# Sparse attention and two expert layers on one core: batch 0's softmax statistics for two heads at a time

## The chip, the cores and the metric

The kernel runs on one core of one Trainium2 chip. The metric is the device time of one execution in microseconds. Three runs of the kernel before took 711.41, 712.30 and 712.85 us, a median of 712.3 us.

## The reference

Inputs are in float32 for q, k, v (2 batches, 8 heads, 576 rows, 64 columns); the weights of the two layers behind the attention follow. The attention keeps in each row only the scores within tau of the row's largest:

```python
scores = scale * np.matmul(q, k.transpose(0, 1, 3, 2))
thresh = np.max(scores, axis=-1, keepdims=True) - tau
scores = np.where(scores >= thresh, scores, -1000000000.0)
scores = scores - np.max(scores, axis=-1, keepdims=True)
attn = np.exp(scores)
attn = attn / (np.sum(attn, axis=-1, keepdims=True) + 1e-09)
return np.matmul(attn, v).astype(np.float32)
```

Its output, 1152 tokens of 512 numbers, goes through a layer `max(x @ w1, x @ w2, x @ w3) @ w_out` and then through four experts of 1024 hidden units, whose outputs are summed with the normalised probabilities of each token.

## The kernel before

The program has two halves. Batch 0's attention comes first and alone on TensorE (`attention_fast`, L531); the products of the two layers (L1192) start behind it, and batch 1's attention (`attention_slow`) is woven into them piece by piece. The change is in `attention_fast` and in the functions that it calls.

**Tiles.** Batch 0 has four jobs, each a pair of heads. A job has nine tiles (`job_steps`, L322): 128 rows of scores against 576 keys, for four chunks of rows and two heads, and one tile with the 64 remaining rows of both heads (`st.h` is None there). The tiles of a chunk follow one another, head 0 and then head 1 (its `mate`), and share one buffer `em`. The 36 tiles are numbered through, from 0. Jobs 0 and 3 have the remainder before their last two tiles, jobs 1 and 2 at their start, so the remainders are tiles 6, 9, 18 and 33.

**One tile.** `qk` (L344) puts the scores into `s` in PSUM, four matmuls of 288 columns; there are two such buffers. `peak` (L369) takes the row's negated maximum on VectorE, `limit` (L376) the threshold from it, on one column. `power` (L379) takes the exponential on ScalarE, into `em`. `weigh` (L383) masks it on VectorE by comparing `s` with the threshold, and sums the row; with it the score buffer is free. `norm` (L389) takes the reciprocal of the sum on VectorE and multiplies the row with it on GpSimd (the last tiles on VectorE). `turn` (L399) transposes the tile on TensorE, four transposes into `t` (two buffers), and for a chunk's second head or a remainder a fifth into `tm`. `cut_hi`, `cut_lo` and `cut_late` split the transposed tile into a high and a low part: in mode "pe" (head 0) by ScalarE, a second set of transposes, a product with the negative identity (L456) and ScalarE again, in mode "pool" (head 1) by a copy on ScalarE and two operations on GpSimd, for a remainder on VectorE. `gather` (L467) multiplies with the values when a group of chunks is complete. `prep` (L198) prepares the next job's keys and queries, one step at each call of `advance`.

**Order.** The loop at L557 writes these steps in program order, for tile `i`: its maximum, the reciprocal of tile `i - 1`, the scores of `i + 1`, the exponential, threshold and mask of `i`, the transposes of `i - 1`, with the splitting of `i - 2` in between. In this half a scheduler then orders each engine's instructions by its own estimate of times; behind it the order on TensorE, VectorE, ScalarE and GpSimd is the program's. Each engine works through its list in order and waits where an operand is not there.

In the listing, the names of buffers are those of the profile: `st_negm`, `st_thr`, `st_sum`, `st_r` are the four columns of a tile (L373).

Of the kernel before, what the change touches and what calls it, by code (L numbers as in the profile page):

```python
# [11 lines left out]
F32 = mybir.dt.float32  # L12
# [3 lines left out]
ALU = mybir.AluOpType  # L16
# [6 lines left out]
def fused_kernel(ctx: ExitStack, tc: tile.TileContext, q, k, v, tau, w1, w2, w3, w_out, probs, m_w1, m_w2, out):  # L23
    nc = tc.nc
# [3 lines left out]
    E, _, F2 = m_w1.shape  # L28
    P = 128
# [28 lines left out]
    SWIFT = 2  # L58
# [3 lines left out]
    CALM, NEARLY = 3, 6  # L62
# [82 lines left out]
    def atile(shape, dt, tag):  # L145
        return at["pool"].tile(shape, dt, tag=tag, name=tag, bufs=at["bufs"].get(tag, 1))

    def ptile_at(x, shape):
        return at[x].tile(shape, F32, tag=x, name=x.lower())

    def load_job(job, names="qkv"):
        b, p = job.b, job.p
        for nm, src in (("q", q), ("k", k), ("v", v)):
            if nm not in names:
                continue
            heads = src[b, 2 * p:2 * p + 2]
            load = nc.scalar.dma_start if nm == "v" and b else nc.sync.dma_start
            main = heads[:, 0:MAIN, :].rearrange("h (p c) d -> p h c d", c=NC)
            if nm == "v":
                t = atile([P, 2, NC, D], F32, "vnat")  # L160
                load(out=t, in_=main)
            else:
                t = atile([P, NC, 2, D], F32, f"{nm}nat")
                for h in range(2):
                    nc.sync.dma_start(out=t[:, :, h, :], in_=main[:, h])
            if nm == "q":
                r = diagonal
                for h in range(2):
                    last = nc.sync.dma_start(out=r[h * REM:(h + 1) * REM, h * D:(h + 1) * D], in_=heads[h, MAIN:S, :])
            elif nm == "k":  # L170
                r = atile([REM, 2, D], F32, "knrem")
                last = nc.sync.dma_start(out=r, in_=heads[:, MAIN:S, :].rearrange("h r d -> r h d"))
            else:
                r = atile([P, D], F32, "vnrem")
                last = load(out=r, in_=heads[:, MAIN:S, :])
            job.raw[nm] = (t, r)
        return last
# [13 lines left out]
    def spin(ps, n):  # L191
        for _ in range(n):
            nc.tensor.matmul(ps, lhsT=still[:, 0:P], rhs=still, start=True, stop=True)  # L193
# [128 lines left out]
    def job_steps(job):  # L322
        steps = []
        late = job.b == 0 and job.p in (0, NPAIR - 1)
        groups = (((0, 1), False), ((2, 3), True))
        for chunks, with_rem in groups if late else groups[::-1]:
            grp = Step()
            grp.job, grp.chunks = job, chunks
            grp.nn = len(chunks) * P
            grp.n = grp.nn + (REM if with_rem else 0)  # L330
            grp.am = [None, None]

            tiles = [(ci, c, h) for ci, c in enumerate(chunks) for h in range(2)]
            if with_rem:
                tiles.insert(-2 if late else 0, (None, None, None))
            for ci, c, h in tiles:
                st = Step()
                st.grp, st.ci, st.c, st.h, st.last = grp, ci, c, h, False
                st.mate = steps[-1] if h else None
                steps.append(st)  # L340
            steps[-1].last = True
        return steps
# [26 lines left out]
    def peak(st):  # L369

        st.em = st.mate.em if st.mate else atile([P, 2 * S], F32, "em")
        st.col = (st.h or 0) * S
        st.stat = {x: atile([P, 1], F32, f"st_{x}") for x in ("negm", "thr", "sum", "r")}  # L373
        nc.vector.tensor_reduce(out=st.stat["negm"], in_=views(st)[0], op=ALU.max, axis=AX.XY, negate=True)  # L374

    def limit(st):  # L376
        nc.vector.tensor_scalar(out=st.stat["thr"], in0=st.stat["negm"], scalar1=-1.0, scalar2=ntau, op0=ALU.mult, op1=ALU.add)

    def power(st):  # L379
        sv, _, ev = views(st)  # L380
        return nc.scalar.activation(out=ev, in_=sv, func=AF.Exp, bias=st.stat["negm"])  # L381

    def weigh(st):  # L383

        sv, _, ev = views(st)
        nc.vector.scalar_tensor_tensor(  # L386
            out=ev, in0=sv, scalar=st.stat["thr"], in1=ev, op0=ALU.is_ge, op1=ALU.mult, accum_out=st.stat["sum"])

    def norm(st, swift=False):  # L389
        em = views(st)[1]  # L390
        su, re = st.stat["sum"], st.stat["r"]
        nc.vector.reciprocal(out=re, in_=su)  # L392
        last = (nc.vector if swift else nc.gpsimd).tensor_scalar(out=em, in0=em, scalar1=re, scalar2=one, op0=ALU.mult, op1=ALU.mult)  # L393
        if st.h is None:
            nc.gpsimd.tensor_scalar(
                out=st.em[:, S:S + REM], in0=st.em[:, MAIN:S], scalar1=1.0, scalar2=1.0, op0=ALU.mult, op1=ALU.mult)
        return last

    def turn(st):  # L399
        st.t = ptile_at("T", [P, NC, P])  # L400
# [62 lines left out]
    def cut_late(st):  # L463
        if st.mode == "pe":
            st.late()
# [65 lines left out]
    def attention_fast(jobs, modes):  # L531

        steps = lined_up(jobs)
        n = len(steps)
        front, back = Queue(), Queue()
        spin(ptile_at("S", [P, 2, 512])[:, 0, 0:SPUN], SPINS)
        load_first(jobs[0])
        stream.flush(-55000)
        load_job(jobs[0], "v")
        start = prep_first(jobs[0])  # L540
        next(start)
        qk(steps[0])
        for _ in start:
            pass
        stream.flush(-READY)
        back.add(values(jobs[0]))

        def advance():

            with ExitStack() as held:  # L550
                if "raised" in at:
                    held.enter_context(tc.issue_after(at["raised"].ins))
                front.advance()
                back.advance()

        urgent = ExitStack()
        for i in range(n + 3):  # L557
            st = steps[i] if i < n else None
            nxt = steps[i + 1] if i + 1 < n else None
            old = steps[i - 2] if 0 <= i - 2 < n else None  # L560
            if st and st.j + 1 < len(jobs):
                if st.r == 0:
                    load_job(jobs[st.j + 1], "v" if st.j else "qkv")
                if st.r == 1 and st.j == 0:
                    front.add(prep(jobs[1]))
                if st.r == AHEAD_A and st.j + 2 < len(jobs):
                    load_job(jobs[st.j + 2], "qk")
            if st:
                peak(st)
            if 0 <= i - 1 < n - 1:  # L570
                norm(steps[i - 1], i - 1 >= n - SWIFT)
            if nxt:
                if nxt.r == 0:
                    front.drain()
                    back.add(values(nxt.job))
                qk(nxt)
                if nxt.r == 0 and nxt.j + 1 < len(jobs):
                    front.add(prep(jobs[nxt.j + 1]))
                if i < len(SPINS_A):
                    with tc.issue_after(nxt.whole.ins):  # L580
                        spin(ptile_at("U", [P, SPUN]), SPINS_A[i])
            if st and not nxt:
                power(st)
                limit(st)
                weigh(st)
                at["normed"] = norm(st, True)
                turn(steps[i - 1])
                urgent.enter_context(tc.issue_after(at["normed"].ins))
            if old:
                cut_hi(old, next(modes) if old.h is not None and i - 2 < n - CALM else "dve")  # L590
            advance()
            if nxt:
                at["raised"] = power(st)
                if i == n - NEARLY:
                    at["nearly"] = at["raised"]
            if old:
                cut_lo(old)
            if nxt:
                limit(st)
            advance()  # L600
            if nxt:
                weigh(st)
                if i:
                    turn(steps[i - 1])
            if st and not nxt:
                at["turned"] = turn(st)
            if old:
                cut_late(old)
                if old.last:
                    back.add(gather(old.grp, i - 2 == n - 1))  # L610
            advance()
            yield
        back.drain()
        urgent.close()
        at["fourth"] = at["stacked"]
# [611 lines left out]
    bufs_a = {"K12": 2, "QS": 2, "V": 2, "VR": 2, "em": 3, "am": 6, "ar": 4}  # L1227
    bufs_b = {"sraw": 2, "K12": 2, "QS": 2, "em": 2, "am": 4, "ar": 2}
    for bf in (bufs_a, bufs_b):
        bf.update({f"st_{x}": 6 for x in ("negm", "thr", "sum", "r")})  # L1230

    layer_max(0)
    MAX0 = plan.cols
# [105 lines left out]
```

## Time and profile before

| | |
|---|---|
| median of three runs | 712.3 us |
| lowest and highest run | 711.41 and 712.85 us |
| profiled execution, its own time | 713.38 us |
| its span from the first to the last instruction | 711.6 us |
| TensorE busy | 693.5 us, 97% |
| VectorE busy | 470.5 us, 66% |
| ScalarE busy | 359.3 us, 50% |
| GpSimd busy | 494.7 us, 70% |

The busy shares are means over the whole program. In the page's 40 slices of 17.8 us the digit of VectorE is 6 in the first slice, then 8, 9, 9, 8, 9, that of TensorE 7 and then 9 throughout; the granted clock of TensorE is 8 tenths in the first slice and 9 or more from the second. Batch 0's attention lies in the first six slices. Instruction times below are in microseconds from the start of the span. VectorE's instructions are pipelined a little: the next one starts before the end of the one before, so the step from start to start is shorter than the duration.

### The profile page before, as it was taken

How to read it: one execution, taken by the hardware profiler on the slowest of the kernel's cores; microseconds unless marked ns; L12 is line 12 of the kernel's file. 1: busy time of each engine (PE TensorE's matmuls, PEld its weight loads, DVE VectorE, ACT ScalarE, POOL GpSimd, SP SyncE). 2: the span in 40 equal slices, each digit the busy share in tenths (PEclk: the TensorE clock that was granted, in tenths of full speed). 3: DMA queues.
4: the chain of work that ended last, by engine and by line, in shares of the span. 5: the costliest groups of instructions: out<-in, count | busy, mean ns of one | idle time of the engine just before them, and what ended most of it. 6: DMA issues, size and time to landing. Idle time of an engine off the chain costs nothing.

```text
span 711.6 us, 11870 instructions
## 1 busy us (share of the span) xinstructions
PE 693.5 (97%) x3961; PEld 613.8 (86%) x3961; DVE 470.5 (66%) x1050; ACT 359.3 (50%) x760; POOL 494.7 (70%) x575
## 2 busy tenths in 40 slices
PE   7999999999899999999999999999999999999997
PEld 7878888877688888888878889999998998998996
DVE  6899898776476676677666477874744644643653
ACT  5788875553454465464555344446524433434430
POOL 5769976876585665675676567789479669669650
PEclk8999999999999999999999999999999999999999
DMA  6763507987978358365333544443232223222203
GB/s 190 177 145 83 152 1 201 277 228 225 238 196 215 119 154 214 106 167 155 119 103 97 178 169 149 148 157 125 60 90 72 78 87 90 87 65 90 56 1 75
DMA packets 108176, 95.04 MB, mean 134 GB/s; under 512 B 26708, under 2 KB 91220, under 8 KB 108116
## 3 DMA queue, kind: packets, MB, share of 16 engines
q1 hardware_dynamic: 90218, 81.14, 40.6%
q10 hardware_dynamic: 17866, 13.14, 6.5%
q8 instruction: 32, 0.52, 0.3%
q14 instruction: 28, 0.23, 0.1%
q0 software_dynamic: 32, 0.00, 0.0%
HBM read 68.96 MB, written 13.37 MB: 116 GB/s over the span
## 4 chain that ended last, share of the span: by engine, by line
PE 84%; ACT 4%; POOL 3%; DVE 3%; DMA 2%; issue 2%; SPq 0%; ACTq 0%; DVEq 0%; POOLq 0%
PE ps L1192 69%; PE u L482 5%; PE s L363 4%; PE t L403 3%; DMA K<-KN 1%; ACT em L381 1%; POOL a L717 1%; PE u L193 1%; DMA krem<-in_k_dram 1%; DVE em L386 1%; ACT a L713 1%; POOL em L393 1%; DVE st_negm L374 1%; ACT am L436 1%; DMA raw<-in_moe_w_dram 0%
## 5 line engine op out<-in xcount | busy, mean ns | idle before, releaser
L1192 PE MATMUL ps<-b,hh 128*128 128x512 f32 (+1 forms) x584 | 185.4, 391 | 2.0 <-POOL b L717 2.0
L717 POOL TENSOR_TENSOR b<-raw,b 128x512 fp32r<-128x512 f32 x64 | 82.9, 1301 | 73.2 <-ACT b L713 72.5
L1192 PEld LDWEIGHTS ps<-b,hh 128*128 128x128 f32 x584 | 108.5, 188 | 23.6 <-POOL b L717 2.9
L1192 PE MATMUL ps<-b,hl 128*128 128x512 f32 (+1 forms) x292 | 114.4, 392 | 0.0
L717 POOL TENSOR_TENSOR a<-raw,a 128x512 fp32r<-128x512 f32 (+1 forms) x57 | 71.7, 1259 | 40.8 <-ACT a L713 40.0
L1156 DVE SCALAR_TENSOR_TENSOR acc<-ps,pr,acc 128x512 f32<-128x512 f32 (+1 forms) x64 | 47.4, 741 | 72.5 <-PE ps L1192 72.3
L393 POOL TENSOR_SCALAR em<-em,st_r,one 128x576 f32<-128x576 f32 x70 | 57.6, 824 | 40.5 <-DVE st_r L392 34.0
L381 ACT ACTIVATE em<-s,st_negm 128x576 f32<-128x576 f32 x72 | 53.6, 744 | 63.3 <-DVE st_negm L374 62.8
L1192 PE MATMUL ps<-y0h,a 128*128 128x512 f32 x256 | 84.1, 400 | 0.0
L374 DVE TENSOR_REDUCE st_negm<-s 128x1 f32<-128x576 f32 x72 | 54.3, 755 | 36.6 <-PE s L363 36.0
L1192 PE MATMUL ps<-bt,sh 128*128 128x320 f32 x300 | 69.9, 309 | 0.0
L386 DVE SCALAR_TENSOR_TENSOR em<-s,st_thr,em 128x576 f32<-128x576 f32 x72 | 58.6, 813 | 10.4 <-ACT em L381 8.1
L977 POOL TENSOR_TENSOR sl<-s,sh 128x512 fp32r<-128x512 f32 x50 | 64.8, 1316 | 0.0
L1192 PEld LDWEIGHTS ps<-b,hl 128*128 128x128 f32 x292 | 55.0, 188 | 10.2
L713 ACT ACTIVATE a<-raw 128x512 fp32r<-128x512 f32 (+1 forms) x66 | 39.7, 604 | 42.7 <-DVE raw L757 13.6
L964 POOL TENSOR_TENSOR dl<-wraw,dh 128x512 fp32r<-128x512 f32 (+1 forms) x50 | 50.0, 1022 | 11.3 <-ACT dh L959 6.9
L1083 ACT ACTIVATE hh<-ps 128x320 fp32r<-128x320 f32 x64 | 27.4, 438 | 54.5 <-DVE ps L1010 54.5
L1192 PEld LDWEIGHTS ps<-y0h,a 128*128 128x128 f32 x256 | 47.4, 189 | 8.5
L1192 PE MATMUL ps<-y0l,a 128*128 128x512 f32 x128 | 51.3, 401 | 0.0
L1192 PEld LDWEIGHTS ps<-bt,sh 128*128 128x128 f32 x300 | 51.1, 188 | 0.0
L363 PE MATMUL s<-K,QS 128*128 128x288 f32 x264 | 49.0, 309 | 1.3 <-DVE em L386 0.6
L970 ACT ACTIVATE sh<-s 128x512 fp32r<-128x512 f32 x50 | 29.9, 625 | 32.9 <-POOL s L909 32.9
(218 smaller groups left out, 1740.5 us busy)
## 6 DMA issues: line engine op xcount, KB each, us to landing
raw<-in_moe_w_dram SPq DMA_DIRECT2D x96, 256.0 KB
words<-in_moe_w_dram SPq DMA_DIRECT2D x18, 512.0 KB
wraw<-in_moe_w_dram SPq DMA_DIRECT2D x16, 512.0 KB
kept_w<-raw SPq DMA_DIRECT2D x18, 256.0 KB
wraw<-kept_w SPq DMA_DIRECT2D x9, 512.0 KB
K<-KN SPq DMA_DIRECT2D x14, 288.0 KB
K<-KN SPq DMA_DIRECT2D x14, 256.0 KB
sraw<-kept_w ACTq DMA_DIRECT2D x14, 256.0 KB
```

The lines of the kernel that those rows point to most:

```text
L363: st.whole = nc.tensor.matmul(st.s[:, kh, 0:HS], lhsT=l, rhs=r, start=i == 0, stop=i == len(terms) - 1)
L374: nc.vector.tensor_reduce(out=st.stat["negm"], in_=views(st)[0], op=ALU.max, axis=AX.XY, negate=True)
L381: return nc.scalar.activation(out=ev, in_=sv, func=AF.Exp, bias=st.stat["negm"])
L386: nc.vector.scalar_tensor_tensor(out=ev, in0=sv, scalar=st.stat["thr"], in1=ev, op0=ALU.is_ge, op1=ALU.mult, accum_out=st.stat["sum"])
L393: last = (nc.vector if swift else nc.gpsimd).tensor_scalar(out=em, in0=em, scalar1=re, scalar2=one, op0=ALU.mult, op1=ALU.mult)
L482: at["valued"] = nc.tensor.matmul(pv, lhsT=l, rhs=r, start=i == 0, stop=i == len(terms) - 1)
L713: nc.scalar.activation(out=b["hi"], in_=b["raw"], func=AF.Copy)
L717: eng.tensor_tensor(out=b["lo"], in0=b["raw"], in1=f32(b["hi"]), op=ALU.subtract)
L964: nc.gpsimd.tensor_tensor(out=rows(b["dl"], x), in0=src, in1=f32(rows(b["dh"], x)), op=ALU.subtract)
L977: nc.gpsimd.tensor_tensor(out=rows(b["sl"], slice(x, x + 2)), in0=rows(b["s"], slice(x, x + 2)), in1=f32(rows(b["sh"], slice(x, x + 2))), ...
L1156: nc.vector.scalar_tensor_tensor(out=accs[t][:, cols], in0=ps, scalar=pe, in1=accs[t][:, cols], op0=ALU.mult, op1=ALU.add)
L1192: nc.tensor.matmul(banks[x], lhsT=l, rhs=r, start=i == 0, stop=i == count - 1)
```

## The change

Tiles go in rounds. A round is one chunk's two heads, or one tile where a pair can't be made: tile 0, tile 1, the remainders, and the last two tiles. The four columns of a tile become tiles of two columns (`sp_negm`, `sp_thr`, `sp_sum`, `sp_r`), one column for each head. In a round of two, VectorE takes both maxima, one threshold on both columns, both masks and one reciprocal on both columns; ScalarE's exponentials and GpSimd's multiplications stay one for each tile. The scores of the tile two places ahead are written behind each mask, and transposing and splitting of the two tiles before go into the same round. `norm` is left to batch 1; the multiplication alone is now `divide`.

```diff
-        st.stat = {x: atile([P, 1], F32, f"st_{x}") for x in ("negm", "thr", "sum", "r")}
+        if not st.stat:
+            st.stat = {x: atile([P, 1], F32, f"st_{x}") for x in ("negm", "thr", "sum", "r")}
...
+        def rounds():
+            i = 0
+            while i < n:
+                size = 2 if 0 < i < n - 2 and steps[i].h == 0 else 1
+                yield steps[i:i + size]
+                i += size
+
+        def follow(i):
...
+            st = steps[i]
+            if st.r == 0:
+                front.drain()
+                back.add(values(st.job))
+            qk(st)
...
+        for unit in rounds():
...
+            stat = {x: atile([P, 2], F32, f"sp_{x}") for x in ("negm", "thr", "sum", "r")}
+            both = {x: t[:, 0:len(unit)] for x, t in stat.items()}
+            for k, st in enumerate(unit):
+                st.stat = {x: t[:, k:k + 1] for x, t in stat.items()}
+                peak(st)
+                if i == 0:
+                    follow(1)
+                at["raised"] = power(st)
...
+            for k, st in enumerate(prev):
+                divide(st, i - len(prev) + k >= n - SWIFT)
+            nc.vector.tensor_scalar(out=both["thr"], in0=both["negm"], scalar1=-1.0, scalar2=ntau, op0=ALU.mult, op1=ALU.add)
+            if last:
+                weigh(unit[0])
+                nc.vector.reciprocal(out=both["r"], in_=both["sum"])
+                at["normed"] = divide(unit[0], True)
+            for k in range(max(len(unit), len(prev))):
+                if k < len(prev):
+                    turn(prev[k])
...
+                    cut_first(prev[k], i - len(prev) + k)
+                advance()
+                if k < len(unit) and not last:
+                    weigh(unit[k])
+                    follow(i + k + 2)
+                if k < len(prev):
+                    cut_lo(prev[k])
+                advance()
...
+                if k < len(prev):
+                    cut_second(prev[k])
+                advance()
+            if not last:
+                nc.vector.reciprocal(out=both["r"], in_=both["sum"])
+            i, prev = i + len(unit), unit
```

What this makes of the engines' lists is shown at three places.

VectorE around tiles 13 to 16, before (`x` and `ar` are results of a gather and of a split):

```order
L374 TENSOR_REDUCE st_negm<-s 128x1 x2
L377 TENSOR_SCALAR st_thr<-st_negm,ntau 128x1 x2
L386 SCALAR_TENSOR_TENSOR em,st_sum<-s,st_thr,em 128x576
L487 TENSOR_TENSOR x_742<-u,pvlo 64x320
L392 RECIPROCAL st_r<-st_sum 128x1
L386 SCALAR_TENSOR_TENSOR em,st_sum<-s,st_thr,em 128x576
L374 TENSOR_REDUCE st_negm<-s 128x1
L461 TENSOR_TENSOR ar<-u,ar 128x128
L392 RECIPROCAL st_r<-st_sum 128x1
L377 TENSOR_SCALAR st_thr<-st_negm,ntau 128x1
L374 TENSOR_REDUCE st_negm<-s 128x1
L386 SCALAR_TENSOR_TENSOR em,st_sum<-s,st_thr,em 128x576
```

and now, tiles 14 to 17:

```order
L376 TENSOR_REDUCE sp_negm<-s 128x1 x2
L615 TENSOR_SCALAR sp_thr<-sp_negm,ntau 128x2
L388 SCALAR_TENSOR_TENSOR em,sp_sum<-s,sp_thr,em 128x576 x2
L466 TENSOR_TENSOR ar<-u,ar 128x128
L639 RECIPROCAL sp_r<-sp_sum 128x2
L376 TENSOR_REDUCE sp_negm<-s 128x1 x2
L615 TENSOR_SCALAR sp_thr<-sp_negm,ntau 128x2
```

Where maxima, thresholds and masks of neighbouring tiles alternated, both maxima now come ahead of the common threshold and both masks behind it.

TensorE in the same stretch, before, with the scores of tiles 15, 16 and 17 (L403 and L406 transpose, L449 and L456 split, L482 is a gather):

```order
L363 MATMUL s<-K_317,QS 128x288 x4
L403 MATMUL t<-ident,em 128x128 x4
L449 MATMUL t<-ident,em 128x128 x4
L363 MATMUL s<-K_317,QS 128x288 x4
L406 MATMUL u<-ident,em 128x128
L456 MATMUL t<-am,nident 128x512
L403 MATMUL t<-ident,em 128x128 x4
L482 MATMUL u<-am,V 128x320 x4
L482 MATMUL u<-ar,VR 128x320
L482 MATMUL u<-am,V 128x320 x4
L363 MATMUL s<-K_317,QS 128x288 x4
```

and now, where the first row holds the scores of tiles 14 and 15:

```order
L364 MATMUL s<-K_327,QS 128x288 x8
L408 MATMUL t<-ident,em 128x128 x4
L454 MATMUL t<-ident,em 128x128 x4
L411 MATMUL u<-ident,em 128x128
L364 MATMUL s<-K_327,QS 128x288 x4
L461 MATMUL t<-am,nident 128x512
L408 MATMUL t<-ident,em 128x128 x4
L487 MATMUL u<-am,V 128x320 x4
L487 MATMUL u<-ar,VR 128x320
L364 MATMUL s<-K_327,QS 128x288 x4
```

Nine transposes stand between the scores of tile 15 and those of tile 16, which take the buffer that the mask of tile 14 frees.

ScalarE around the exponentials of tiles 14 to 17, now (L383; the first row holds two):

```order
L383 ACTIVATE em<-s,sp_negm 128x576 x2
L441 ACTIVATE am<-t 128x4x128
L445 ACTIVATE ar<-u 128x128
L462 ACTIVATE am<-t 128x4x128
L383 ACTIVATE em<-s,sp_negm 128x576
L438 ACTIVATE tcopy<-t 128x512
L383 ACTIVATE em<-s,sp_negm 128x576
L490 ACTIVATE pvlo<-u 64x320
```

The exponentials of tiles 14 and 15 are neighbours; between those of 16 and 17 stands a copy of a transposed tile.

## Rows read from the trace of the kernel before

**Rows 1.** Busy time in windows: window, length, busy us (instructions) of each engine, PEclk, DMA share, GB/s
```profile
50.00:60.00 10.00, 9.89 (x73) 9.26 (x73) 9.51 (x30) 9.06 (x21) 9.71 (x13) 1.00 0.17 38
60.00:70.00 10.00, 8.82 (x62) 7.18 (x61) 9.54 (x27) 8.81 (x21) 9.45 (x15) 1.00 0.54 122
```

**Rows 2.** The chain that ended last, 10 to 107 us, shares by line
```profile
by line: PE u L482 14.7%; PE s L363 12.0%; PE t L403 8.0%; issue 7.9%; ACT em L381 7.2%; PE u L193 5.8%; DVE em L386 4.2%; ACT am L436 3.8%; POOL em L393 3.4%; DMA K<-KN 3.2%; DVE st_negm L374 3.2%; PE t L449 2.5%; PE t L456 2.3%; PE ps L11
```

**Rows 3.** VectorE's instructions in order of time: start us, us, instruction [idle before]
```profile
90.65 0.80 DVE L386 SCALAR_TENSOR_TENSOR em<-s,st_thr,em 128x576 f32<-128x576 f32 x1
91.39 0.07 DVE L386 DVE_READ_ACCUMULATOR em<-s,st_thr,em 128x1 f32 x1
91.39 0.20 DVE L377 TENSOR_SCALAR st_thr<-st_negm,ntau 128x1 f32<-128x1 f32 x1
91.51 0.14 DVE L392 RECIPROCAL st_r<-st_sum 128x1 f32<-128x1 f32 x1
...
97.08 0.75 DVE L374 TENSOR_REDUCE st_negm<-s 128x1 f32<-128x576 f32 x1
97.75 0.15 DVE L392 RECIPROCAL st_r<-st_sum 128x1 f32<-128x1 f32 x1
97.82 0.40 DVE L487 TENSOR_TENSOR x<-u,pvlo 64x256 f32<-64x256 f32 x1
```

**Rows 4.** VectorE in order of time, two pairs of dependent neighbours
```profile
66.45 0.20 DVE L377 TENSOR_SCALAR st_thr<-st_negm,ntau 128x1 f32<-128x1 f32 x1
66.65 0.82 DVE L386 SCALAR_TENSOR_TENSOR em<-s,st_thr,em 128x576 f32<-128x576 f32 x1
...
92.88 0.76 DVE L374 TENSOR_REDUCE st_negm<-s 128x1 f32<-128x576 f32 x1 [0.17 <-PE s L363]
93.67 0.21 DVE L377 TENSOR_SCALAR st_thr<-st_negm,ntau 128x1 f32<-128x1 f32 x1
```

**Rows 5.** TensorE in order of time around tile 27's scores
```profile
77.89 0.69 PE L363 MATMUL s<-K,QS 128*128 128x288 f32 x4
78.42 0.60 PE L449 MATMUL t<-ident,em 128*128 128x128 f32 x4
78.86 0.27 PE L406 MATMUL u<-ident,em 128*128 128x128 f32 x1
78.89 0.48 PE L456 MATMUL t<-am,nident 128*128 128x512 f32 x1
79.20 0.60 PE L403 MATMUL t<-ident,em 128*128 128x128 f32 x4
80.17 0.79 PE L363 MATMUL s<-K,QS 128*128 128x288 f32 x4 [0.36 <-DVE em L386]
```

**Rows 6.** VectorE in order of time in the same stretch
```profile
78.62 0.76 DVE L374 TENSOR_REDUCE st_negm<-s 128x1 f32<-128x576 f32 x1 [0.89 <-PE s L363]
...
80.03 0.08 DVE L386 DVE_READ_ACCUMULATOR em<-s,st_thr,em 128x1 f32 x1
```

**Rows 7.** TensorE in order of time, a gather of 256 columns
```profile
92.68 0.63 PE L482 MATMUL u<-am,V 128*128 128x256 f32 x4
93.15 0.28 PE L482 MATMUL u<-ar,VR 128*128 128x256 f32 x1
93.27 0.70 PE L363 MATMUL s<-K,QS 128*128 128x288 f32 x4
```

**Rows 8.** TensorE's waits, 10 to 104 us: waited for, us in total, times, longest us
```profile
PE t L403 <- POOL em L393: 0.6, 1, 0.6
PE s L363 <- DVE em L386: 0.6, 2, 0.4
```

**Rows 9.** ScalarE's groups, 10 to 104 us: count, busy us, mean ns, idle before
```profile
L381 ACT ACTIVATE em<-s,st_negm 128x576 f32<-128x576 f32 x36 | 26.9, 748 | 3.8 <-DVE st_negm L374 3.3
L436 ACT ACTIVATE am<-t 128x512 fp32r<-128x512 f32 (+1 forms) x25 | 12.8, 528 | 3.3 <-PE t L403 3.0
```

**Rows 10.** The chain in order of time behind the stage: start us, us, what
```profile
106.91 51.30 PE ps L1192 x249
```

More of the change, by code (lines that the diff above doesn't have):

```diff
@@ L339, in job_steps @@
                 st.mate = steps[-1] if h else None
+                st.stat = None
                 steps.append(st)
@@ L387, in weigh, with divide @@
             out=ev, in0=sv, scalar=st.stat["thr"], in1=ev, op0=ALU.is_ge, op1=ALU.mult, accum_out=st.stat["sum"])
-    def norm(st, swift=False):
+    def divide(st, swift=False):
         em = views(st)[1]
-        su, re = st.stat["sum"], st.stat["r"]
-        nc.vector.reciprocal(out=re, in_=su)
+        re = st.stat["r"]
         last = (nc.vector if swift else nc.gpsimd).tensor_scalar(out=em, in0=em, scalar1=re, scalar2=one, op0=ALU.mult, op1=ALU.mult)
@@ L397, in norm @@
         return last
+    def norm(st):
+        nc.vector.reciprocal(out=st.stat["r"], in_=st.stat["sum"])
+        divide(st)
     def turn(st):
@@ L554, in advance @@
                 back.advance()
-        urgent = ExitStack()
[L557 to L568, printed above, removed]
-                peak(st)
[L570 to L592, printed above, removed]
@@ new lines, in rounds @@
+        def rounds():
[5 more added lines that the diff above has]
+        def follow(i):
+            if i >= n:
+                return
+            st = steps[i]
[3 more added lines that the diff above has]
+            qk(st)
+            if st.r == 0 and st.j + 1 < len(jobs):
+                front.add(prep(jobs[st.j + 1]))
+            if i - 1 < len(SPINS_A):
+                with tc.issue_after(st.whole.ins):
+                    spin(ptile_at("U", [P, SPUN]), SPINS_A[i - 1])
@@ new lines, in cut_first, with cut_second @@
+        def cut_first(st, i):
+            cut_hi(st, next(modes) if st.h is not None and i < n - CALM else "dve")
+        def cut_second(st):
+            cut_late(st)
+            if st.last:
+                back.add(gather(st.grp, st is steps[-1]))
+        urgent = ExitStack()
+        i, prev = 0, []
+        for unit in rounds():
+            last = unit[-1] is steps[-1]
+            for st in unit:
+                if st.j + 1 < len(jobs):
+                    if st.r == 0:
+                        load_job(jobs[st.j + 1], "v" if st.j else "qkv")
+                    if st.r == 1 and st.j == 0:
+                        front.add(prep(jobs[1]))
+                    if st.r == AHEAD_A and st.j + 2 < len(jobs):
+                        load_job(jobs[st.j + 2], "qk")
+            stat = {x: atile([P, 2], F32, f"sp_{x}") for x in ("negm", "thr", "sum", "r")}
+            both = {x: t[:, 0:len(unit)] for x, t in stat.items()}
+            for k, st in enumerate(unit):
+                st.stat = {x: t[:, k:k + 1] for x, t in stat.items()}
+                peak(st)
+                if i == 0:
+                    follow(1)
@@ L593, in attention_fast @@
                 at["raised"] = power(st)
-                if i == n - NEARLY:
+                if i + k == n - NEARLY:
                     at["nearly"] = at["raised"]
[L596 to L610, printed above, removed]
@@ L611, in attention_fast @@
-            advance()
-            yield
+            for k, st in enumerate(prev):
[8 more added lines that the diff above has]
+                    turn(prev[k])
+                    if last and k + 1 == len(prev):
+                        urgent.enter_context(tc.issue_after(at["normed"].ins))
+                    cut_first(prev[k], i - len(prev) + k)
[6 more added lines that the diff above has]
+                advance()
+                if last and k + 1 == len(prev):
+                    at["turned"] = turn(unit[0])
+                if k < len(prev):
+                    cut_second(prev[k])
+                advance()
@@ L613, in attention_fast @@
+            if not last:
+                nc.vector.reciprocal(out=both["r"], in_=both["sum"])
+            i, prev = i + len(unit), unit
+            yield
+        cut_first(prev[0], n - 1)
+        advance()
+        cut_lo(prev[0])
+        advance()
+        cut_second(prev[0])
         back.drain()
@@ L1229, in fused_kernel @@
     for bf in (bufs_a, bufs_b):
-        bf.update({f"st_{x}": 6 for x in ("negm", "thr", "sum", "r")})
+        bf.update({f"s{y}_{x}": 6 for x in ("negm", "thr", "sum", "r") for y in "tp"})
     layer_max(0)
```

## The prediction, made before the changed kernel ran

> **What bounds the kernel now.** The page's engine shares point at TensorE, but the change touches only batch 0's attention, so I read that stretch, from 10 us to where the weight products run without a break, at 107 us [rows 10]. First the busy time in windows of 10 us: two windows of the stretch show two different limits. Between 50 and 60 us TensorE is busy 9.89 of 10, between 60 and 70 us VectorE 9.54 against TensorE's 8.82 [rows 1]. Then the chain of waits that ended last, cut to this stretch: the reader is to see that TensorE's lines lead it (gather products L482, scores L363, transposes L403), and that VectorE's two lines with a share, the mask L386 and the maximum L374, hold 4.2% and 3.2%; threshold and reciprocal are too small to appear [rows 2]. So VectorE is full enough to matter, but it is mostly not what ends last. Behind 107 us TensorE runs 249 matmuls in 51.30 us with nothing else in the chain [rows 10]: a shift of the stage's end is handed on, and I carry it to the end of the program undiminished.
>
> **What is removed.** Of 36 tiles 28 form 14 pairs (the first tile, its mate, the four remainder tiles and the last two stay alone). So 14 thresholds and 14 reciprocals go. What counts on VectorE is not an instruction's duration but the step from its start to the next start: a threshold 91.39 to 91.51, 0.12 us, a reciprocal 97.75 to 97.82, 0.07 us [rows 3]. 14 x 0.19 = 2.66 us of VectorE time: the upper bound of the gain, nothing the lower. I take the part where VectorE is the limit or close to it: five pairs lie between 40 and 70 us in the new order, 5 x 0.19 = **-0.95 us**. A second column is entered at nothing: 0.67 us for a maximum over 576 columns [rows 3] is 0.001 us each.
>
> [...]
>
> **What is added: neighbours that depend on each other.** The threshold now follows the second maximum, in most pairs with nothing between. A maximum with an unrelated follower takes 0.67 us to the next start (97.08 to 97.75) [rows 3], with its own threshold behind it 0.79 (92.88 to 93.67) [rows 4]; a threshold with its own mask behind it 0.20 instead of 0.12 (66.45 to 66.65) [rows 4]. In the five pairs where I counted a gain, three have nothing between maximum and threshold, all five nothing between threshold and mask: 3 x 0.12 + 5 x 0.08 = **+0.76 us**. Nearly all of the gain there is given back.
>
> **What is moved: the mask of the first head.** This is the step that I expect to decide. A score buffer (two exist) is free when its mask is done. Before, the mask of a tile needs only its own maximum. Now the first head's mask stands behind the second head's maximum and the common threshold. So after the pair's second score product TensorE has to wait for the first score product of the next pair: 0.04 us to the maximum (a score product ends 77.89 + 0.69, the maximum starts 78.62) [rows 5, 6], 0.79 to the threshold, 0.20 to the mask [rows 4], 0.73 + 0.08 for the mask and its sum [rows 3, 6], 0.06 to the product (80.11 to 80.17) [rows 5, 6]: **1.90 us**. That is free as long as TensorE has 1.90 us of other work placed between those two products. The order of the new kernel shows what stands there; the steps are 0.44 us for four transposes, 0.31 for the product with the negative identity [rows 5], 0.47 and 0.12 for a gather's four and one [rows 7], more in proportion to 320 columns, 0.11 for a single transpose. Tiles are numbered from 0. Pair 4/5 has 1.43 us there, 14/15 0.99, 19/20 1.41, 21/22 1.84, 27/28 1.73, 29/30 1.59, 31/32 1.45; the other seven have 2.0 or more. The missing pieces are 0.47 + 0.91 + 0.49 + 0.06 + 0.17 + 0.31 + 0.45 = 2.86 us. TensorE's waits for a mask in the old trace, 0.6 us in all [rows 8], are of the same kind and go: **+2.26 us** net. Bounds: -0.6 us if TensorE is always late anyway, +2.86 if nothing is saved.
>
> [...]
>
> **Other moves.** Both divisions on GpSimd now wait for the second head's sum, and the transposes behind them are a round later; the old trace shows one wait of TensorE for a division, 0.6 us [rows 8]. I enter nothing for this, with 0.6 us to either side. ScalarE's second exponential can start later when a copy of the previous pair stands between the two (see the rivals); forecast: hidden. SP's queue keeps its number of transfers, and prep steps are called as often per tile, so loads are entered at nothing; if a K transfer came late, the 3.2% that one has in the chain [rows 2] would grow.
>
> **Sum.** -0.95 + 0.76 + 2.26 = +2.07 us. Against the profiled execution, 713.38 us, that is 715.5. That execution lay 1.1 us over the median of the runs, 712.3, so the forecast in the runs' terms is **714.4 us**, slower by 0.3%. About 0.2%, 1.4 us, is what a measurement of this kernel can tell from no change.
>
> **Rivals.**
> *Faster: VectorE was the limit after all.* For it: 9.5 of 10 busy in both windows [rows 1]. Against it: its small share in the chain [rows 2]. If TensorE's missing work is filled by work that is late anyway, all 2.66 us come off: 709.6 us. Adding the 0.6 us of old waits gives 709.0, the low end. [...] Chance 0.28.
>
> *No change.* TensorE's work per tile is untouched, and where it is full [rows 1] neither a lighter VectorE nor a wait covered by its backlog shows. It decides if TensorE runs at least a microsecond behind at the pairs named above. 712.3 us, within 1.4 either way. Chance 0.25. [...]
>
> *Much slower: ScalarE delays the second head.* The first exponential ends 0.75 + 0.04 + 0.75 = 1.54 us after the first maximum starts; a copy of 0.53 us behind it [rows 9] ends 2.07 us after it, and the second exponential 0.75 later at 2.82, while VectorE could start the second mask at 0.67 + 0.79 + 0.20 + 0.73 = 2.39. That is 0.4 us late, and the order has such a copy between the exponentials of ten of the 14 pairs. It decides when the copy's own input is there before the second maximum ends. 10 x 0.4 = 4.0 on top of the forecast: 718.4 us, the high end. Chance 0.17.
>
> **How the numbers follow.** The forecast itself, slower by 1.4 to 4 us, has 0.30 and is the likeliest; its own range is 713.7 to 716.3. With the much slower case, slower by over 0.2% has 0.47; within 0.2% has 0.25; faster by over 0.2% has 0.28. The range from 709.0 to 718.4 runs from the full gain to the full delay on ScalarE; I leave under 0.2 outside, for a stage whose four engines fit together worse or better than the bounds say.
>
> **What would show it.** In the new profile 22 thresholds and 22 reciprocals must stand in batch 0, with durations as now. Right would be: TensorE's idle time in front of score products, put down to the mask, grows from 0.6 to some 3 us before 110 us, mostly at the pairs named, and the uninterrupted products start some 2 us later than 107. VectorE's idle time before maxima grows alike, since those wait for the products. Wrong in its main step: that wait stays near 0.6 us and the start moves earlier (then the faster rival), or VectorE's waits for exponentials grow by some 4 us (the ScalarE rival). If the stage's end moves and the total does not follow, the handing on behind 107 us was wrong.

## The result and the profile after

The changed kernel takes 720.12 us (median of four runs, 718.66 to 720.48), the kernel before 712.17 in the same comparison: a ratio of 1.0100 with a 95% interval from 1.0082 to 1.0117, **slower by about 7 us** (the two medians lie 8.0 us apart). The direction was forecast; 714.4 was not, and 720.1 lies above the range (709.0 to 718.4). The profiled execution took 720.45 us with a span of 718.7, against 713.38 and 711.6.

The loss lies in batch 0's attention and is handed on. The chain of waits behind the stage, in order of time (start us, us, what), beside [rows 10]:

```profile
114.06 38.15 PE ps L1226 x193
```

TensorE's unbroken products begin at 114.06 us instead of 106.91, 7.1 us later, and the span is 7.1 us longer. In the stage TensorE is less busy than before; the window in which it falls most, in the columns of [rows 1]:

```profile
50.00:60.00 10.00, 7.84 (x60) 7.20 (x59) 8.49 (x21) 7.22 (x14) 8.17 (x11) 1.00 0.15 35
```

TensorE fell from 9.89 to 7.84 of 10 and VectorE from 9.51 to 8.49 at the same granted clock (1.00). Summed from 10 to 110 us it is 86.2 us against 93.4 for TensorE and 87.7 against 91.6 for VectorE. Both wait more, and for each other. TensorE's waits from 10 to 114 us (waited for: us in total, times, longest us), beside [rows 8]:

```profile
PE s L364 <- DVE em L388: 5.1, 9, 1.3
PE t L408 <- POOL em L394: 2.9, 3, 1.8
PE t L461 <- ACT am L441: 1.2, 3, 0.6
PE u L487 <- DVE ar L466: 1.1, 1, 1.1
```

The wait for the mask in front of score products grew from 0.6 to 5.1 us (forecast: some 3), that for divisions from 0.6 to 2.9. VectorE's waits in the same stretch, and before the change (10 to 104 us):

```profile
DVE sp_negm L376 <- PE s L364: 4.9, 7, 1.2
DVE em L388 <- ACT em L383: 1.7, 2, 1.0
```
```profile
DVE st_negm L374 <- PE s L363: 2.5, 6, 0.9
DVE em L386 <- ACT em L381: 1.7, 4, 0.6
```

Maxima wait 4.9 us for score products (2.5 before); masks wait for exponentials as long as before, 1.7 us. The surprise stands among VectorE's groups (count, busy us, mean ns, idle before), after and, in the last line, before:

```profile
L615 DVE TENSOR_SCALAR sp_thr<-sp_negm,ntau 128x2 f32<-128x2 f32 x14 | 6.0, 426 | 0.4
L639 DVE RECIPROCAL sp_r<-sp_sum 128x2 f32<-128x2 f32 x14 | 2.2, 157 | 0.1
L615 DVE TENSOR_SCALAR sp_thr<-sp_negm,ntau 128x1 f32<-128x1 f32 x8 | 1.7, 208 | 0.0
L639 DVE RECIPROCAL sp_r<-sp_sum 128x1 f32<-128x1 f32 x7 | 1.1, 155 | 0.1
```
```profile
L377 DVE TENSOR_SCALAR st_thr<-st_negm,ntau 128x1 f32<-128x1 f32 x36 | 7.3, 206 | 0.2
```

A second column costs the reciprocal 2 ns. It makes the threshold twice as long: 14 x (426 - 208) ns = 3.1 us more than at one column. VectorE has 28 instructions fewer in the whole program and is not less busy (471.5 us, 470.5 before). The longest of TensorE's waits shows where that lands; VectorE, GpSimd and TensorE in order of time (start us, us, instruction):

```profile
93.74 1.40 DVE L376 TENSOR_REDUCE sp_negm<-s 128x1 f32<-128x576 f32 x2
95.17 0.76 DVE L615 TENSOR_SCALAR sp_thr<-sp_negm,ntau 128x2 f32<-128x2 f32 x1
96.03 0.82 DVE L388 SCALAR_TENSOR_TENSOR em<-s,sp_thr,em 128x576 f32<-128x576 f32 x1
96.78 0.08 DVE L388 DVE_READ_ACCUMULATOR em<-s,sp_thr,em 128x1 f32 x1
```
```profile
95.08 1.64 POOL L394 TENSOR_SCALAR em<-em,sp_r,one 128x576 f32<-128x576 f32 x2
```
```profile
95.42 0.27 PE L411 MATMUL u<-ident,em 128*128 128x128 f32 x1
97.00 1.29 PE L364 MATMUL s<-KN,QD 128*128 128x288 f32 x8 [1.31 <-DVE em L388]
```

These are tiles 31 and 32, a pair that the prediction named, and the remainder, tile 33. Two maxima, the threshold, the first mask, and only then the next scores: the chain that was forecast. The threshold in it ends at 95.93, when GpSimd's first division of 0.82 us (95.08 to 95.90) does.

### The profile page after: what moved, and what is told of

The parts are those of the page before. It is cut to its first block, busy times and chain, and to the rows that moved or that the text cites. A ratio compares the mean times of both kernels' runs of the same rounds, so it can differ in the third digit from the quotient of the medians.

```text
span 718.7 us, 11835 instructions
## 1 busy us (share of the span) xinstructions
PE 692.8 (96%) x3961; PEld 612.1 (85%) x3961; DVE 471.5 (66%) x1022; ACT 360.4 (50%) x760; POOL 495.2 (69%) x575
## 4 chain that ended last, share of the span: by engine, by line
PE 84%; DVE 4%; ACT 3%; POOL 2%; issue 2%; DMA 2%; SPq 0%; ACTq 0%; POOLq 0%; DVEq 0%
PE ps L1226 70%; PE u L487 5%; PE s L364 4%; PE t L408 3%; DVE em L388 1%; DVE sp_negm L376 1%; DMA krem<-in_k_dram 1%; POOL em L394 1%; DMA QS<-qnat 1%; ACT em L383 1%; DMA raw<-in_moe_w_dram 0%; ACT am L441 0%; PE t L454 0%; PE t L461 0%; PE u L233 0%
## 5 line engine op out<-in xcount | busy, mean ns | idle before, releaser
L383 ACT ACTIVATE em<-s,st_negm 128x576 f32<-128x576 f32 x36 | 26.7, 741 | 59.8 <-DVE st_negm L376 59.8
L394 POOL TENSOR_SCALAR em<-em,st_r,one 128x576 f32<-128x576 f32 x36 | 29.8, 829 | 34.5 <-DVE st_r L401 28.4
L376 DVE TENSOR_REDUCE st_negm<-s 128x1 f32<-128x576 f32 x36 | 27.3, 758 | 32.7 <-PE s L364 32.4
L364 PEld LDWEIGHTS s<-K,QS 128*128 128x128 f32 x264 | 40.3, 191 | 9.6 <-DVE em L388 2.5
L408 PE MATMUL t<-ident,em 128*128 128x128 f32 x288 | 43.5, 273 | 4.4 <-POOL em L394 4.4
```

The source lines that it names most:

```text
L364: st.whole = nc.tensor.matmul(st.s[:, kh, 0:HS], lhsT=l, rhs=r, start=i == 0, stop=i == len(terms) - 1)
L408: last = nc.tensor.transpose(st.t[:, j, :], st.em[:, off + j * P:off + (j + 1) * P], ident)
```

## The experiments

Theories: **P**, a threshold of more than one column waits for GpSimd (first written down for an even number of columns only, with three back at 0.21 us); **D**, it is long because it follows the maximum that it needs; **W**, the first mask behind the second maximum is the loss, as forecast; **R**, the common reciprocal comes too late for GpSimd; **O**, the order that the scheduler makes of the new source, taken as a whole. Every ratio is to runs of the kernel before on the same chip. V, S and T are explained in the expectations that use them.

**One number changed: two columns or three.** In the changed kernel, and apart from it in the kernel before. The added columns are zeros that nobody reads, and a single tile of the changed kernel keeps one column (shortened):

```diff
-  out=both["thr"], in0=both["negm"]
+  out=thrs[:, o:o + 2], in0=negs[:, o:o + 2]    (control)
+  out=thrs[:, o:o + 3], in0=negs[:, o:o + 3]    (second run)
```

> The changed kernel with maxima and thresholds in two fixed tiles (rows of four columns) in place of rotating ones; every instruction in the same order, the pair's threshold on two columns. It is the control for the next run. All theories: as the changed kernel, 720 us within 1 us, the 14 two-column thresholds at a mean near 0.43 us.

> As the control, with the pair's threshold on three columns (the third is a zero that nobody reads): one number differs, the order of instructions doesn't. [...] Theory D (the threshold is long because it stands behind the second maximum, whose result it needs): 0.43 us stay and the time stays within 0.7 us. Theory W (TensorE's waits for the first mask are nearly all of the loss): the thresholds may fall, the time moves by less than 1.5 us.

> The kernel before, unpaired, but each of batch 0's 36 thresholds works on two columns (the second is a zero that nobody reads). Nothing new waits for anything. Theory P: the mean rises from 0.21 to about 0.4 us, longest where GpSimd works, 36 x 0.2 = 7 us of VectorE time, and the kernel is 2 to 7 us slower than before. Theory D: 0.21 us stay, the time is within 0.7 us of before.

> As the run with two columns on the kernel before, in the same order, with three columns. Theory P: thresholds back at 0.21 us and the time within 1 us of before (what the slightly other order is worth is all that is left). Theory D, and a rival by which every further column costs: as with two columns or worse.

Control 1.0097 (1.0081 to 1.0114), with three columns 1.0089 (1.0071 to 1.0107); the kernel before with two 1.0129 (1.0111 to 1.0147), with three 1.0130 (1.0108 to 1.0151). In the changed kernel the thresholds took 351 ns in the control, less than the 0.43 us expected, and 363 with three columns. VectorE's groups in the kernel before with two, and with three columns:

```profile
L388 DVE TENSOR_SCALAR thrs<-negs,ntau 128x2 f32<-128x2 f32 x36 | 16.6, 474 | 0.1
```
```profile
L388 DVE TENSOR_SCALAR thrs<-negs,ntau 128x3 f32<-128x3 f32 x36 | 17.4, 496 | 0.1
```

D falls: here nothing was paired, and the thresholds grew from 206 to 474 ns. "Even" falls too: three columns are as slow as two. The step is from one column to more than one. Whether it is a wait for GpSimd is read from the two engines in order of time, in the kernel before with two columns:

```profile
18.39 0.83 DVE L388 TENSOR_SCALAR thrs<-negs,ntau 128x2 f32<-128x2 f32 x1
...
25.40 0.22 DVE L388 TENSOR_SCALAR thrs<-negs,ntau 128x2 f32<-128x2 f32 x1
...
61.58 1.52 DVE L388 TENSOR_SCALAR thrs<-negs,ntau 128x2 f32<-128x2 f32 x1
```
```profile
17.91 1.28 POOL L730 TENSOR_TENSOR a<-raw,a 128x512 fp32r<-128x512 f32 x1 [0.62 <-ACT a L726]
...
60.55 1.28 POOL L465 TENSOR_TENSOR am<-tcopy,am 128x512 fp32r<-128x512 f32 x1
61.80 1.28 POOL L304 TENSOR_TENSOR V<-vnat,V 128x512 fp32r<-128x512 f32 x1
```

The threshold of 18.39 ends at 19.22, GpSimd's operation at 19.19. That of 61.58 ends at 63.10, after two operations of GpSimd, 61.83 and 63.08. At 25.40 GpSimd was idle, and the threshold took 0.22 us. The seven of the 36 that meet no GpSimd operation at all took 0.21 to 0.23 us; each of the 21 over 0.3 us ends within 0.04 us of the end of a GpSimd operation. P is shown, without its word "even". Why the threshold on one column (206 ns) is spared and those on two and three (474 and 496 ns) are not, no run shows.

**The same threshold by other means.**

```diff
-  nc.vector.tensor_scalar(out=both["thr"], in0=both["negm"], scalar1=-1.0, scalar2=ntau, ...)
+  nc.vector.tensor_tensor(out=both["thr"], in0=ntau2[:, 0:len(unit)], in1=both["negm"], op=ALU.subtract)
```

> The changed kernel with the pair's threshold formed by another instruction, still one on two columns: a column pair that holds minus tau, less the column pair of negated maxima (the same numbers). TensorE's and ScalarE's orders are the changed kernel's but for one moved row each, VectorE's but for a few neighbours. The changed kernel's 14 two-column thresholds took 6.0 us, 3.0 more than 14 x 0.21. Theory P (a threshold of more than one column in its old form waits until GpSimd's running operation ends): if this form doesn't wait, thresholds come down to about 0.2 us, TensorE's wait for masks in front of score products falls from 5.1 to about 2.5 us, and the time falls from 720.1 to 716 to 717.5. Theory W (the first mask behind the second maximum is nearly all of the loss): not below 718.8. If this form waits as well, the thresholds stay near 0.43 us and the time at 720.

1.0120 (1.0103 to 1.0136), no gain. This form waits as well, and even on one column, where it has two inputs of one column each in SBUF:

```profile
L618 DVE TENSOR_TENSOR sp_thr<-ntau,sp_negm 128x2 f32<-128x2 f32 x14 | 4.0, 285 | 0.4
L618 DVE TENSOR_TENSOR sp_thr<-ntau,sp_negm 128x1 f32<-128x1 f32 x8 | 3.2, 399 | 0.0
```

At one column it took 399 ns in the mean. The two of the eight beside an idle GpSimd took 151 and 159 ns, and of the other six, 0.18 to 0.98 us long, five end within 0.02 us of the end of a GpSimd operation. The run could not separate P from W, since it did not take the wait away.

**Parts undone, with the scheduler free.** Five runs undo parts of the pairing in the source (edits shortened).

```diff
two thresholds
-            nc.vector.tensor_scalar(out=both["thr"], in0=both["negm"], ...)
+            for st in unit:
+                limit(st)
only the reciprocal common: the loop over the pair takes in the maxima
-            for k, st in enumerate(unit):
-                peak(st)
-                at["raised"] = power(st)
...
+            for k in range(max(len(unit), len(prev))):
+                peak(unit[k])
+                at["raised"] = power(unit[k])
+                limit(unit[k])
...
                 weigh(unit[k])
own reciprocals
                 weigh(unit[k])
+                nc.vector.reciprocal(out=unit[k].stat["r"], in_=unit[k].stat["sum"])
...
-            nc.vector.reciprocal(out=both["r"], in_=both["sum"])
```

The order of the pair alone is the first edit with the third, and the run with nothing common the second with the third.

> The changed kernel with two one-column thresholds in the place of each common one: pairs, order of the source and the common reciprocal stay, the order that the scheduler makes shifts somewhat. Theory P: thresholds at 0.21 us, time 716 to 718, in spite of 14 more instructions. Theory W: the first mask still stands behind the second maximum, so 719 to 720.5.

> The changed kernel with each head's threshold and first mask in front of the second head's maximum, as before the change; only the reciprocal is still common to the pair, and divisions and transposes wait for the second head as in the changed kernel. Theory P and W together (slow threshold and late first mask are the whole loss): 712 to 714 us, and TensorE's wait for masks near 0.6 us. Theory R (a good part is the late reciprocal: GpSimd waits 5.7 us for it, TensorE 2.9 us for divisions): 715 to 717.5, with GpSimd's wait for reciprocals still at 5 us or so.

> The changed kernel with a reciprocal for each head right behind its mask (14 more instructions); the common threshold stays. Theory R: GpSimd's wait for reciprocals falls from 5.7 to 3 us or less, TensorE's wait for divisions from 2.9 to about 1, time 717 to 718.5. Theories P and W: within 0.8 us of 720.1, since the common threshold and the late first mask remain.

> The changed kernel with nothing in pairs but the order: both maxima, two one-column thresholds, the first mask and its reciprocal, the second mask and its reciprocal; as many VectorE instructions as before the change. Theory W (the first mask behind the second maximum costs most): 716.5 to 719, TensorE's wait for masks in front of scores 3 us or more. Theory R (the common reciprocal): at most 715, since no reciprocal is late any more.

> The run with only the reciprocal in common, with a reciprocal for each head as well: nothing is shared by the pair, what is left of the change is the new way in which the source is written (both heads' divisions, transposes and splitting in one round). All theories: TensorE's wait for masks near 0.6 us. Theory R: 712 to 713, the 2.5 us of the run with the common reciprocal gone. Rival S (the source's new order of the other steps costs the rest): 714 to 715.5, as with the common reciprocal.

| run | ratio to before | 95% interval |
|---|---|---|
| two thresholds | 1.0097 | 1.0082 to 1.0113 |
| only the reciprocal common | 1.0036 | 1.0023 to 1.0048 |
| own reciprocals, common threshold | 1.0115 | 1.0098 to 1.0131 |
| order of the pair alone | 1.0030 | 1.0019 to 1.0040 |
| nothing common | 1.0082 | 1.0066 to 1.0097 |

These don't add up under any of the theories. The order alone costs 2.1 us, with this wait of TensorE, some 3 us as forecast. That it is so near the +2.07 of the prediction proves nothing, since its order is another than the changed kernel's:

```profile
PE s L364 <- DVE em L388: 3.4, 6, 0.8
```

The run with only the reciprocal common, where each head's mask stands in front of the second maximum again, has the wait for masks back at 0.6 us. It still loses 2.6 us, with 2.6 us of waits for divisions. But the run in which nothing is common, no pair at all, loses 5.8 us, more than the one that still shares the reciprocal. Every edit gave the scheduler another start, and it made another order on all engines; in the unpaired run TensorE waits 2.8 us for masks, 1.9 for ScalarE's copies, and 1.5 in front of one score product, put down to a threshold. So these five runs tell only that the scheduler's order is worth several us by itself. It had to be held.

**Parts undone, every engine's order held.** Each engine's order in the changed kernel was written into the program, as edges between neighbours that set the order and wait for nothing else; the added instructions stand right behind the one that they were split from, a first head's reciprocal right behind its mask. In the traces TensorE, ScalarE and GpSimd then run the changed kernel's list instruction by instruction. The last run does the same with the order of the kernel before. No run holds an order and changes nothing else, so the price of the holding itself is not measured.

```diff
+        for x, y in zip(row, row[1:]):
+            tc.add_manual_dep(y, x.name, mybir.DependencyInfo(mybir.DependencyClass.NoSync, mybir.DependencyReason.DATA), reason="order")
```

> The changed kernel with every engine's order held as it is, and each pair's common threshold split into two one-column thresholds next to each other (14 more instructions). Theory P (the common threshold's waits for GpSimd, 3.0 us, are on the path): thresholds at 0.21 us, 716.5 to 718. Theory O (the order itself costs nearly all): 719 to 720.5.

> The changed kernel with every engine's order held, and each pair's common reciprocal split: the first head's stands right behind its mask. Theory R (late divisions): TensorE's waits for divisions fall from 2.9 us to 1 or less, GpSimd's for reciprocals from 5.7 to 3 or less, 717 to 718.5. Theories P and O: 719.3 to 720.8, nothing but 14 more instructions.

> Both splits at once, order held: as many VectorE instructions as before the change, nothing in common between the heads, only the changed kernel's order. Theories P and R together: 714 to 716, what is left is the wait for the first mask that was forecast (2 to 3 us). Theory O: 718 or more, the order that the scheduler made is the main loss, and TensorE's waits for masks stay at 4 us or more.

> The kernel before with every engine's order held, and each of batch 0's 36 thresholds on two columns (the second a zero that nobody reads), as in the earlier run whose order the scheduler had moved a little. Theory P: 36 thresholds at a mean of 0.4 us or more, 718 to 723. Rival S (the earlier run's 9.4 us came from its other order): 713 to 716.

| run, order held | ratio to before | 95% interval |
|---|---|---|
| changed kernel (above; control) | 1.0100; 1.0097 | 1.0082 to 1.0117; 1.0081 to 1.0114 |
| threshold split | 1.0068 | 1.0051 to 1.0086 |
| reciprocal split | 1.0115 | 1.0098 to 1.0131 |
| both split | 1.0065 | 1.0050 to 1.0080 |
| before, thresholds on two columns | 1.0072 | 1.0053 to 1.0091 |

Now it adds up in the main. Splitting the threshold takes off 0.30%, some 2 us, although 14 instructions come back; the runs are from different chips, and the intervals just overlap. On one chip it shows more clearly: with the reciprocal split in both, the common threshold costs 1.0115 against 1.0065, 0.50% or 3.6 us, and these intervals lie apart. So the slow threshold is worth 2 to 3.6 us. Splitting the reciprocal takes off nothing, alone or with the threshold: R finds no support. But it brings TensorE's waits for divisions only from 2.9 to 1.9 and 1.7 us, and GpSimd's for reciprocals only from 5.7 to 4.9 and 5.4; what the rest of them costs stays open. What is left with nothing shared, 0.65% or 4.6 us (3.6 to 5.7), is the order, the first mask behind the second maximum included. TensorE's waits with the threshold split, and with both split:

```profile
PE s L374 <- DVE em L398: 3.0, 8, 0.7
PE t L418 <- POOL em L404: 2.7, 3, 1.7
```
```profile
PE s L374 <- DVE em L398: 3.3, 9, 0.7
PE t L418 <- POOL em L404: 1.7, 2, 1.3
PE t L471 <- ACT am L451: 1.3, 3, 0.7
PE u L497 <- DVE ar L476: 1.1, 1, 1.1
```

Without slow thresholds the wait for masks is 3.0 to 3.3 us, again the size that was forecast, and no single one is over 0.7 us. The last run shows P with nothing else moved: thresholds of 518 ns, 11.1 us more VectorE time, and of that 5.1 us in the result (9.2 us where the scheduler was free), where TensorE's wait for masks went from 0.6 to 5.4 us:

```profile
L397 DVE TENSOR_SCALAR thrs<-negs,ntau 128x2 f32<-128x2 f32 x36 | 18.4, 518 | 0.2
```
```profile
PE s L376 <- DVE em L406: 5.4, 10, 1.2
```

**Is VectorE the limit before the change?** Two runs on the kernel before take thresholds off VectorE:

```diff
-  nc.vector.tensor_scalar(out=st.stat["thr"], ...)
+  nc.scalar.activation(out=st.stat["thr"], in_=st.stat["negm"], func=AF.Identity, bias=ntau, scale=-1.0)   (first run)
-  in0=sv, scalar=st.stat["thr"], in1=ev
+  in0=ev, scalar=floor, in1=ev                                                                           (second run)
```

> The kernel before, unpaired, with batch 0's 36 thresholds moved from VectorE to ScalarE, each behind its exponential. In the run with slow thresholds 9.3 us more of VectorE time made the kernel before 9.4 us longer, so VectorE's time seems to count there one for one. Theory V (it counts in the other direction too): 36 x 0.12 us of steps go, 4.3 us: 708 to 710. Rival T (before the change VectorE and TensorE limit in turn; less VectorE time alone leaves TensorE's share as it is, and the mask waits for ScalarE's extra 0.2 us): 711.5 to 715.

> The kernel before with no threshold at all in batch 0: the mask compares the exponential with exp(-tau), a constant made once, in place of the score with the threshold. Each mask then reads both inputs from SBUF and none from PSUM, and a score buffer is free when its exponential is done. Theory P, widened by the runs (VectorE instructions that need more than one read from SBUF wait for GpSimd's running operation): the masks, 0.81 us now, reach a mean of 1.1 us or more, and 36 x 0.3 = 11 us outweigh the 4.3 us of thresholds: 715 to 722. If masks of this length don't wait: 706 to 710.

The first: 0.9994 (0.9983 to 1.0005), no change with 36 instructions off VectorE. Theory V's 708 to 710 us did not come. But the masks wait for ScalarE in return, 4.8 us instead of 1.7, its thresholds took 302 ns in the mean (rival T counted 0.2 us), and the scheduler's order is another, so V is not refuted as such. The second: 1.0202 (1.0186 to 1.0218). This mask, which reads both inputs from SBUF, waits for GpSimd too; the group now, and before:

```profile
L391 DVE SCALAR_TENSOR_TENSOR em<-em,floor 128x576 f32<-128x576 f32 x36 | 38.0, 1070 | 2.7 <-ACT em L386 2.0 <-PE t L408 0.4
```
```profile
L386 DVE SCALAR_TENSOR_TENSOR em<-s,st_thr,em 128x576 f32<-128x576 f32 x36 | 29.2, 812 | 2.4 <-ACT em L381 1.7 <-issue 0.2
```

Sixteen of the 36 took 0.80 to 0.82 us; of the other 20, all but one end 0.60 to 0.62 us behind the end of a GpSimd operation. That is 36 x (1070 - 812) ns = 9.3 us more VectorE time in place of the 4.3 us of thresholds. The kernel lost more than the difference, 14.4 us. GpSimd's divisions grew as well, from 824 to 1018 ns, and the order moved; the shares were not separated. No run here beats the kernel before.

## Why the prediction was wrong, step by step

- **"A second column is entered at nothing"** is the step that failed. It was worked out from how long 576 columns take, and it holds for the reciprocal (157 and 155 ns). The threshold's second column lets it wait for GpSimd: 3.1 us of VectorE time (2.0 in the control), and with the order held 2 to 3.6 of the 5 us by which the loss, 7.1, exceeds the forecast, 2.07. The trace of before has thresholds of one column only, and the row used in their place, a maximum over 576 columns, is another operation that reads PSUM; it bounded nothing here.
- **-0.95 us where VectorE is the limit**: no run shows it. VectorE's busy time did not fall, and with the order held, 14 reciprocals put back cost nothing (1.0065 with them, 1.0068 without). The Faster rival falls by the result itself. Whether a lighter VectorE gains anything stays open, since the run with 36 thresholds off it (0.9994) paid with waits for ScalarE. A heavier one does cost: 11.1 us more of it gave 5.1 us.
- **+2.26 us for the first mask behind the second maximum** was right in mechanism. TensorE waits for masks 5.1 us in all, 4.5 more than before against 2.26 net. Five of the seven named pairs show it: in front of tiles 6, 21, 23, 29 and 33 there are 0.65, 0.20, 0.62, 0.48 and 1.31 us, 3.26 against 1.64 forecast for the same five. With the threshold split and the order held the five have 0.44, 0.18, 0.20, 0.19 and 0.63 us, 1.64 in all, so the excess was the slow threshold. Pairs 14/15 and 29/30, 0.91 and 0.31 forecast, show none. The remaining four waits, 1.84 us, stand elsewhere; one, 0.68 in front of tile 22, is for a pair's second mask, which the prediction did not count. With one-column thresholds and the pair's order the total is 3.0 to 3.4 us in four runs, 2.4 to 2.8 more than before. For a threshold that does not wait the five pairs were sized right. That the total fits too is partly luck: in that run 0.53 us in front of tile 3 and 0.70 in front of tile 22, neither forecast, stand in for the two pairs that show none.
- **Late divisions at nothing, 0.6 either side**: the wait itself is far above that, 2.9 us of TensorE's time. Splitting the reciprocal, which brings them to 1.9 or 1.7 us, does not shorten the kernel; what the remaining wait costs is not shown.
- **ScalarE delays the second head**: refuted, masks wait 1.7 us for exponentials as before.
- **Handing-on behind 107 us**: held, 7.1 us at the stage's end and 7.1 in the span.
- What the sum also left out is the order as a whole. With nothing shared and the changed kernel's order held 4.6 us remain. The wait for masks there is 2.7 us above that of before; the other 1.9 us stand among waits for divisions (1.1 us more), for ScalarE's `am` and for the remainder's part on VectorE, `ar`. Which of them cost the 1.9 us was not separated. The prediction took the scheduler's order as given at the seven pairs and did not ask what it did elsewhere.

## What to carry to other kernels

Before merging small instructions into a wider one, look at what the wider form needs: on VectorE, one column and two can differ by a wait for another engine (206 and 474 ns here), and the place to see it is not the mean but the end of each long instance beside what GpSimd ends at that moment. Before an instruction saved on a busy engine is entered as a gain, take it away in a run that moves nothing else; busy time alone does not say what it is worth (11.1 us more of it gave 5.1 us here). Where a scheduler sets the order, an edit is measured together with its new order; hold the order before you share out the loss among the parts.

## What was unexpected of the hardware

- A threshold (`tensor_scalar`, float32, SBUF to SBUF) took 0.19 to 0.22 us on one column in all 36 instances before the change, 19 of them wholly within a running GpSimd operation, and 0.20 to 0.21 us in the eight after it, five of them so. On two columns it took 0.21 to 0.23 us beside an idle GpSimd and otherwise mostly ended with GpSimd's running operation; the longest took 1.52 us, behind two operations in a row. The means on two or three columns are 351 to 518 ns. GpSimd's own operations hardly lengthened by it: batch 0's divisions took 827 ns after and 824 before.
- A `tensor_tensor` of two SBUF columns waited even at one column (399 ns mean), and so did a mask with both inputs in SBUF (1070 against 812 ns). Beside such masks GpSimd's divisions lengthened too, from 824 to 1018 ns. The mask that reads PSUM and SBUF did not show it (813 ns after, 812 before, none over 819). A reciprocal on two SBUF columns did not wait either (157 ns, none over 167).
